# Two transformer layers on one core: where V's token tiles are projected, how the first chunk's reciprocal is cut, and where the second chunk's heads are split

## The chip, the cores and the metric

One Trainium2 chip, one of its cores. The metric is the device time of one launch in microseconds (us), the median of several runs; less is better. Engines are named as in the profile: PE is TensorE, DVE is VectorE, ACT is ScalarE, POOL is GpSimd, SP is SyncE.

## The reference

The input x is 2048 tokens by 512, in float32. The same two blocks are applied twice, with the same weights (two layers):

```
x = x + A(layernorm(x))     # A: q,k,v = x @ wqkv (32 heads of 16); softmax(q k^T / 4) v; @ wo
x = x + B(layernorm(x))     # B: mish(x @ w1 + b1) @ w2, hidden width 1792
```

Weights are wqkv 512 x 1536, wo 512 x 512, w1 512 x 1792, w2 1792 x 512, all float32.

## The kernel before

**Numbers.** Products with weights are made of three float32r matmuls each (`mm3`, L196 to L201): the operands are split into a high and a low half, and high x high, high x low and low x high are added up. A tile of 128 tokens by 512 outputs thus takes 4 x 3 matmuls of 128x512.

**Stages of a layer.** (1) `qkv` (L555) projects Q and K, feature tile by feature tile, for four chunks of 512 tokens, and writes them to DRAM (`scr`); from there `prep_qk` (L341) loads the rows of four heads at a time into the blocks `ks` and `qs`. Then it projects V (`v_parts`, L619): 16 tiles of 128 tokens, each in 4 parts (one for each 128 rows of the weight, three matmuls). Two tiles share a block `v` that GpSimd presets to 1 (L624), ScalarE evicts into it (L638), and SyncE writes each tile to DRAM (`vscr`, L642, 512 KB). `prep_v` (L370) loads the V rows of a group of four heads from there into `va`, in four pieces. (2) The attention (`Attention.run`, L506). (3) Output projection, the residual and the second layer norm. (4) The MLP. Activations between the layers lie in DRAM.

**The attention.** 512 steps (and 4 more to empty the pipeline): 8 groups of 4 heads, 4 chunks of 512 queries, 16 tiles of 128 keys. A step's scores are four 128x512 matmuls with 50 rows: 48 for the three-part product and 2 that subtract the row maximum. Scores are taken in threes: a pair (P: L452, one exponential of 128x1024 at L453) and a single (S: L462, exponential of 128x512 at L463). The row maxima are made ahead of the scores: a half max step (M, `max_mm`, L378) is two 128x512 matmuls into a pair of PSUM banks (`pm`, L400) and a DVE maximum over 128x1024 (L404). After each 16 max steps `max_fold` (L408) folds them: two small DVE operations (L413, L417), two GpSimd casts (high and low half, L421, L423), two writes to DRAM by SyncE (`nd`, L422, L424) and four transfers from there into the rows of `qs` (L427). The scores of those 16 steps need these rows. Small v in the cycle below is a pv matmul group (L478). Three steps make a cycle:

```python
CYCLE = ("PMvSM", "PvMSPMv", "SMPvMS")
```

PE's order is pinned as one chain. DVE, ACT, POOL and SP issue in order too; calls under `behind` keep program order there, the rest is placed by the scheduler. The maxima run `AHEAD` = 21 steps ahead of the scores. To get there, `qkv` runs `AHEAD + PRE` = 25 max steps between its matmuls (`some_max`): 12 in the Q/K part, 13 behind each third V part. It projects V's tiles 0 to 11 (48 parts); tiles 12 to 15 (16 parts) are projected by the attention itself in the first `2 * PRE` = 8 M places, two parts in each (L523), which are steps 0 to 3. The order of M places ends 21 steps before the scores; from there the tail runs without maxima.

**Blocks.** One pool of 22 blocks of 8 KB a partition holds nearly everything: weights, transposed inputs, `ks`, `qs`, `va`, `v`, the probabilities `p` (one block for a pair and a single), and, in the tail, the numerators and reciprocals. A block is given to its next owner in turn, so that an owner waits for the readers of the one before.

**Weights kept.** In layer 0, at step `KEEP` = 2, `keep_all` writes the six split blocks of wqkv to DRAM through GpSimd's queue (L144, 1 MB each), for layer 1.

**The end of the attention.** `HeadsOut` works on one chunk of 512 queries at a time: `load` brings numerator and denominator back from DRAM (L661), `invert` takes the reciprocal of the denominator (128x128, DVE, L664) and writes it out (POOL, L666), `spread` loads it over the heads' rows into the block `rec` (POOL, L672), `parts` multiplies (DVE, 128x2048, L676), casts the high half (POOL, L679) and subtracts for the low half (DVE, L680). The schedule at L886 hangs these on steps, counted from the end: chunk 0 at -42 (load), -38 (invert), -36 (spread), -20 (parts); chunk 1 at -29, -21, -20, -13; chunk 2 at -13, -9, -8. Behind the attention (L897 to L920) come the load of chunk 3, `parts` of chunk 2, and the output projections (`wo_parts`, L698) of chunks 0, 1, 2, with the layer norm of chunk 0 between them.

Of the kernel before, what the change touches and what calls it, by code (L numbers as in the profile page):

```python
# [38 lines left out]
QW = CW // 4  # L39
TR = 32  # L40
AHEAD = 21
PRE = 4
KEEP = 2
PREP = 2
WARM = (4, 1, 1)
# [1 line left out]
STEPS = NG * GSTEPS  # L47
# [31 lines left out]
def kernel(ctx: ExitStack, tc: tile.TileContext, x, wqkv, wo, w1, b1, w2, out):  # L79
# [48 lines left out]
    def behind(ins):  # L128
        return tc.keep_in_program_order(ins)
# [194 lines left out]
    class Attention:  # L324
# [181 lines left out]
        def run(self, hooks, pre):  # L506
            self.prep_v(0, range(NCH - 1))
            left = 2 * PRE
            close_banks()
            with tc.tile_pool(name="sa", bufs=1, space=PSUM, reuse_waits="tile") as self.pool:  # L510
                half, done = 2 * (AHEAD + PRE), -4
                for s in range(STEPS + 4):
                    if s % GSTEPS == GSTEPS - NKT and s // GSTEPS + 1 < NG:
                        self.prep_v(s // GSTEPS + 1)
                    for item in CYCLE[s % 3]:
                        if item == "P":
                            self.pair()
                            self.drain()
                        elif item == "S":
                            self.single()  # L520
                        elif item == "M" and left:
                            left -= 1
                            next(pre)  # L523
                            next(pre)
                            if not left:
                                next(pre, None)
                                self.prep_v(0, [NCH - 1])
                        elif item == "M":
                            self.max_mm(half // 2, half % 2)
                            half += 1  # L530
# [24 lines left out]
    def qkv(l, att, wts, tt, order, within, due):  # L555
        scr = att.scr
        ahead = [0]

        def some_max():
            if ahead[0] < AHEAD + PRE:  # L560
                for n in range(2):
                    att.max_mm(ahead[0], n)
                ahead[0] += 1

        done = 0
        spare = []
        parts = iter(())
        for n, (m, c) in enumerate(order):
            for fn in within.get((n, 0), []):
                fn()  # L570
            w = wts[m // 2]
            if n % 2:
                if not spare:
                    two = b8([P, 2, 2, CW], F32R, f"pt{l}{m}{c}")
                    spare += [two[:, 0], two[:, 1]]
                pt = spare.pop(0)
            else:
                pt = tmp.tile([P, 2, CW], F32R, tag="raw", name=f"pt{l}{m}{c}", bufs=3)
# [17 lines left out]
            split_psum(pt[:, 0], pt[:, 1], acc)  # L596
            nc.scalar.dma_start(
                scr[m][:, :, ts(c, CW)].bitcast(F32).rearrange("a p n -> p a n"), pt.bitcast(F32)
            )
            for fn in due.get((m, c), []):  # L600
                fn()
            for _ in range(2):
                next(parts, None)
            if m in (0, 4):
                done += 1
                if done == 2 * NCH:
                    parts = att.prep_qk(0)
# [11 lines left out]
    def v_parts(l, c, wts, tt, att, paired):  # L619
        th, tl = tt[c]  # L620
        for t in range(NCH):
            if t % 2 == 0:
                v = b8([P, 2, H, VW], F32, f"v{l}{c}{t}")
                nc.gpsimd.memset(v, 1.0)  # L624
                if paired:
                    pair = ps.tile([P, 2, 512], F32, tag="mx", name=f"vp{l}{c}{t}")
            acc = pair[:, t % 2] if paired else pbank("s", f"va{l}{c}{t}")
            for k in range(KT):
                w = wts[4 + k // 2]
                mm3(  # L630
                    acc,
                    [(th[:, k, ts(t, P)], tl[:, k, ts(t, P)], w[:, 0, k % 2], w[:, 1, k % 2])],
                    first=k == 0,
                    last=k == KT - 1,
                    pe=att.pe,
                )
                yield
            nc.scalar.activation(v[:, t % 2, :, 0:DH], acc.rearrange("p (h d) -> p h d", d=DH), AF.Copy)  # L638
            if t % 2:
                k0 = c * NCH + t - 1  # L640
                for k in range(2):
                    nc.sync.dma_start(  # L642
                        att.vscr[:, :, k0 + k].rearrange("g p n -> p g n"),
                        v[:, k].rearrange("p (g h) d -> p g (h d)", g=NG),
                    )

    class HeadsOut:
        def __init__(self, l, c, src):
# [11 lines left out]
            for h in range(P // DH):  # L660
                nc.sync.dma_start(self.num[ts(h, DH)], rows[:, h, 0:DH].rearrange("k d n -> d k n"))  # L661

        def invert(self):
            behind(nc.vector.reciprocal(self.den, self.den))  # L664
# [9 lines left out]
        def parts(self):  # L674
            nm = f"{self.l}{self.c}"
            behind(nc.vector.tensor_tensor(self.num, self.num, self.rec, op=ALU.mult))  # L676
            oh = b8([P, KT, CW], F32R, "oh" + nm)
            ol = b8([P, KT, CW], F32R, "ol" + nm)
            nc.gpsimd.tensor_copy(oh, self.num)  # L679
            behind(nc.vector.tensor_tensor(ol, self.num, oh.bitcast(F32), op=ALU.subtract))  # L680
            self.out = oh, ol

        def pieces(self):
            nm = f"{self.l}{self.c}"
# [149 lines left out]
    for l in range(2):  # L834
# [39 lines left out]
        def at(s, fn):  # L874
            hooks.setdefault(s, []).append(fn)
# [7 lines left out]
        for i in range(2):  # L883
            at(STEPS - 9 + 2 * i, lambda i=i: wot.append(ready(f"wo{i}", l)))
        outs = [HeadsOut(l, c, att.oscr) for c in range(NCH)]
        for c, (t0, t1, t2, t3) in enumerate(((-42, -38, -36, -20), (-29, -21, -20, -13), (-13, -9, -8, None))):  # L886
            o = outs[c]
            at(STEPS + t0, o.load)
            at(STEPS + t1, o.invert)
# [7 lines left out]
        att.run(hooks, v_parts(l, NCH - 1, wts, tt, att, True))  # L897
# [12 lines left out]
        for i, _ in enumerate(project(1)):  # L910
            for n in range({0: 1, 8: 1, 11: 2, 14: 2}.get(i, 0)):
# [70 lines left out]
```

## Time and profile before

| | |
|---|---|
| median of 3 runs | 3492.14 us (3491.93 to 3492.74) |
| the profiled execution's own time | 3493.51 us |
| its span | 3491.7 us, TensorE clock 1.00 |
| PE busy | 3478.3 us |
| DVE busy | 3001.3 us |
| ACT busy | 2572.9 us |
| POOL busy | 240.2 us |
| V stage of layer 0, layer 1 | 116.40 to 161.27, 1851.68 to 1896.56 |
| attention of layer 0, layer 1 begins | 161.27, 1896.56 |
| first output projection of layer 0 begins | 1400.68 |

All times of rows are microseconds from the span's start. A row of a timeline has start, duration, engine, line, operation, written and read tiles, shapes and count; in brackets stands the idle time of the engine ahead of it and what ended that. A row of the groups by line has count, busy time, mean duration in ns, idle time ahead and its main releasers. A matmul of 128x512 is shown longer than its share of TensorE, since matmuls are pipelined: the distance between starts counts. SPq is SyncE's sequencer issuing transfers.

### The profile page before, as it was taken

How to read it: one execution, taken by the hardware profiler on the slowest of the kernel's cores; microseconds unless marked ns; L12 is line 12 of the kernel's file. 1: busy time of each engine (PE TensorE's matmuls, PEld its weight loads, DVE VectorE, ACT ScalarE, POOL GpSimd, SP SyncE). 2: the span in 40 equal slices, each digit the busy share in tenths (PEclk: the TensorE clock that was granted, in tenths of full speed). 3: DMA queues.
4: the chain of work that ended last, by engine and by line, in shares of the span. 5: the costliest groups of instructions: out<-in, count | busy, mean ns of one | idle time of the engine just before them, and what ended most of it. 6: DMA issues, size and time to landing. Idle time of an engine off the chain costs nothing.

```text
span 3491.7 us, 68687 instructions
## 1 busy us (share of the span) xinstructions
PE 3478.3 (100%) x28572; PEld 1921.3 (55%) x28572; DVE 3001.3 (86%) x3166; ACT 2572.9 (74%) x3513; POOL 240.2 (7%) x392
## 2 busy tenths in 40 slices
PE   9999999999999999999999999999999999999999
PEld 7644444444444444888876444444444444448887
DVE  6689999999999996667756999999999999956675
ACT  3288888888888889356622888888888888884565
POOL 3100010001001002100010000000000000021000
PEclk9999999999999999999999999999999999999999
DMA  7741323222131314722374203111120312156210
GB/s 248 234 91 44 64 60 75 50 53 72 51 63 56 65 36 91 231 69 73 109 224 151 45 21 58 34 35 34 32 48 21 54 27 45 21 113 213 76 37 25
DMA packets 185268, 274.99 MB, mean 79 GB/s; under 512 B 72117, under 2 KB 114037, under 8 KB 171133
## 3 DMA queue, kind: packets, MB, share of 16 engines
q1 hardware_dynamic: 158036, 193.95, 22.8%
q10 hardware_dynamic: 19176, 43.06, 3.6%
q0 software_dynamic: 7744, 33.60, 3.4%
q8 instruction: 224, 3.67, 0.5%
q14 instruction: 88, 0.71, 0.1%
HBM read 158.87 MB, written 110.62 MB: 77 GB/s over the span
## 4 chain that ended last, share of the span: by engine, by line
PE 96%; DMA 1%; DVE 1%; ACT 1%; issue 0%; POOL 0%; SPq 0%; DVEq 0%; ACTq 0%; POOLq 0%
PE pv L478 30%; PE pm L400 18%; PE ss L462 13%; PE sp L452 9%; PE h L733 8%; PE mo L759 8%; PE qk L199 2%; PE qk L200 1%; PE qk L201 1%; PE va L199 1%; PE wo L199 1%; PE wo L201 1%; PE wo L200 1%; PE va L201 1%; PE va L200 1%; DMA vscr<-v 0%
## 5 line engine op out<-in xcount | busy, mean ns | idle before, releaser
L404 DVE TENSOR_REDUCE mxv<-pm 128x2 f32<-128x1024 f32 x2048 | 2384.2, 1218 | 148.4 <-PE pm L400 96.0
L453 ACT ACTIVATE p<-sp 128x1024 f32<-128x1024 f32 x1366 | 1396.5, 1022 | 10.6 <-DMA vscr<-v 2.7
L478 PE MATMUL pv<-p,va 128*32 128x256 f32 (+2 forms) x16032 | 1165.7, 392 | 0.6 <-ACT ot L501 0.4
L400 PE MATMUL pm<-ks,qs 48*128 48x512 f32 x4096 | 1099.0, 446 | 1.6 <-DVE mxv L404 1.3
L463 ACT ACTIVATE p<-ss 128x512 f32<-128x512 f32 x1364 | 815.3, 598 | 338.6 <-PE ss L462 258.1
L452 PE MATMUL sp<-qs,ks 50*128 50x512 f32 x2732 | 738.1, 445 | 0.5 <-ACT p L453 0.5
L478 PEld LDWEIGHTS pv<-p,va 128*32 128x32 f32 x16032 | 368.3, 108 | 504.9 <-issue 424.4
L400 PEld LDWEIGHTS pm<-ks,qs 48*128 48x128 f32 x4096 | 451.8, 184 | 347.2 <-issue 234.1
L462 PE MATMUL ss<-qs,ks 50*128 50x512 f32 x1364 | 610.6, 448 | 1.5 <-ACT p L463 1.5
L462 PEld LDWEIGHTS ss<-qs,ks 50*128 50x128 f32 x1364 | 252.1, 185 | 329.4 <-ACT p L463 238.1
L452 PEld LDWEIGHTS sp<-qs,ks 50*128 50x128 f32 x2732 | 267.0, 183 | 184.4 <-ACT p L453 108.5
L421 POOL CAST hi<-nt 128x32 fp32r<-128x32 f32 x64 | 13.3, 208 | 2263.1 <-DVE nt L417 2263.1
L736 ACT ACTIVATE hb<-h,b1t 128x512 f32<-128x512 f32 x112 | 77.2, 689 | 101.6 <-PE h L733 100.7
L740 ACT ACTIVATE hr<-he 128x512 f32<-128x512 f32 x112 | 70.8, 632 | 104.6 <-DVE he L739 104.6
L193 ACT ACTIVATE pt<-qk 128x512 fp32r<-128x512 f32 x64 | 38.2, 597 | 143.4 <-PE qk L201 102.0
L743 DVE TENSOR_TENSOR hb<-hb,hr 128x512 f32<-128x512 f32 x112 | 77.4, 691 | 45.0 <-ACT hr L741 42.9
L737 DVE TENSOR_SCALAR he<-hb 128x512 f32<-128x512 f32 x112 | 47.5, 424 | 79.8 <-ACT hb L736 73.8
L747 DVE TENSOR_TENSOR al<-hb,ah 128x512 fp32r<-128x512 f32 x112 | 77.4, 691 | 28.8 <-ACT ah L746 23.1
L746 ACT ACTIVATE ah<-hb 128x512 fp32r<-128x512 f32 x112 | 70.2, 627 | 29.9 <-DVE hb L743 29.9
L739 DVE SCALAR_TENSOR_TENSOR he<-he 128x512 f32<-128x512 f32 x112 | 76.7, 685 | 17.2 <-ACT he L738 17.2
L194 DVE TENSOR_TENSOR pt<-qk,pt 128x512 fp32r<-128x512 f32 x64 | 43.8, 685 | 53.7 <-ACT pt L193 51.6
L741 ACT ACTIVATE hr<-hr,lnhalf 128x512 f32<-128x512 f32 x112 | 81.1, 724 | 3.6
(224 smaller groups left out, 3000.5 us busy)
## 6 DMA issues: line engine op xcount, KB each, us to landing
scr<-pt ACTq DMA_DIRECT2D x64, 512.0 KB
qs<-scr SPq DMA_DIRECT2D x174, 128.0 KB
ks<-scr SPq DMA_DIRECT2D x174, 128.0 KB
vscr<-v SPq DMA_DIRECT2D x32, 512.0 KB
va<-vscr SPq DMA_DIRECT2D x64, 256.0 KB
oscr<-ot SPq DMA_DIRECT2D x64, 256.0 KB
ww<-sw POOLq DMA_DIRECT2D x14, 1024.0 KB, 4.3
num<-oscr SPq DMA_DIRECT2D x64, 128.0 KB
```

What stands on the lines that cost most here:

```text
L199: pe(nc.tensor.matmul(acc, ah, bh, start=first and i == 0, stop=False))
L200: pe(nc.tensor.matmul(acc, ah, bl, start=False, stop=False))
L201: pe(nc.tensor.matmul(acc, al, bh, start=False, stop=last and i == n - 1))
L400: nc.tensor.matmul(pm[:, e], qs[u][rows, q0 : q0 + P], ks[u][rows, ts(n, 512)], start=True, stop=True)
L404: nc.vector.tensor_reduce(self.mxs[b][:, 2 * u : 2 * u + 2, qt, n], pm, axis=AX.X, op=ALU.max)
L452: self.pe(nc.tensor.matmul(sp[:, e], k, q, start=True, stop=True))
L453: nc.scalar.activation(self.pts[-1][:, 0:n], sp[:, 0:n], AF.Exp, scale=SCALE)
L462: self.pe(nc.tensor.matmul(sp, k, q, start=True, stop=True))
L463: nc.scalar.activation(self.pts[i // 3][:, 2], sp, AF.Exp, scale=SCALE)
L478: nc.tensor.matmul(self.accs[b][ts(h, VW), cols], self.va[b // NCH][:, kt, h, :], self.pts[j][:, e, cols], start=kt == 0 and q0 == 0, stop ...
L733: pe(nc.tensor.matmul(acc, w[:, part, k, ts(f % 2, P)], t[:, k, :], start=i == 0, stop=i == 3 * KT - 1))
L759: nc.tensor.matmul(obs[c][t // 2][:, t % 2], act[:, ts(t, P)], w[:, part, f % 2], start=f == part == 0 and act is ah, stop=f == FT - 1 and ...
```

## The change

Three parts.

1. `PRE` goes from 4 to 1. The projections now take V's tiles 0 to 14 (60 parts); only tile 15 (4 parts) is left for the attention's first two M places. The maxima run 22 steps ahead in the projections instead of 25: 12 in the Q/K part, 10 in the V part, now behind each fourth part, which is a whole tile. In the attention, maxima therefore begin with the third M place. `v_parts` is one generator over all 16 tiles, evicts and writes a tile before it yields the last part, and takes its PSUM bank from the attention's pairs for tile 15 alone. From step 4 on the order of P, S, M and v is as before.
2. The reciprocal of chunk 0 is cut into four of 128x32, at steps -38 to -35; its writes to DRAM all go with the last; `spread` moves from -36 to -34.
3. `parts` of chunk 1 leaves step -13. Behind the attention come now: the product of chunk 1 and that of chunk 2 (both DVE), then the split of chunk 1 with its cast on ACT instead of POOL, and the subtraction on DVE. The split of chunk 2 (cast on POOL) follows in the middle of the first output projection.

```diff
-PRE = 4
+PRE = 1
...
-                            next(pre)
-                            next(pre)
+                            next(self.pre)
+                            next(self.pre)
                             if not left:
-                                next(pre, None)
                                 self.prep_v(0, [NCH - 1])
...
-        i = 0
-        for c in range(NCH - 1):
-            for _ in v_parts(l, c, wts, tt, att, False):
-                i += 1
-                if i % 3 == 0:
-                    some_max()
+        att.pre = v_parts(l, wts, tt, att)
+        for i in range(NKT * KT - 4 * PRE):
+            next(att.pre)
+            if i % 4 == 3:
+                some_max()
...
+    def v_parts(l, wts, tt, att):
+        for n in range(NKT):
+            c, t = divmod(n, NCH)
+            th, tl = tt[c]
             if t % 2 == 0:
                 v = b8([P, 2, H, VW], F32, f"v{l}{c}{t}")
                 nc.gpsimd.memset(v, 1.0)
-                if paired:
-                    pair = ps.tile([P, 2, 512], F32, tag="mx", name=f"vp{l}{c}{t}")
-            acc = pair[:, t % 2] if paired else pbank("s", f"va{l}{c}{t}")
+            if n < NKT - PRE:
+                acc = pbank("s", f"va{l}{c}{t}")
+            else:
+                acc = ps.tile([P, 2, 512], F32, tag="mx", name=f"vp{l}{c}{t}")[:, 0]
...
-        def invert(self):
-            behind(nc.vector.reciprocal(self.den, self.den))
-            for q in range(NCH):
+        def invert(self, i=0, n=1):
+            part = ts(i, P // n)
+            behind(nc.vector.reciprocal(self.den[:, part], self.den[:, part]))
+            for q in range(NCH if i == n - 1 else 0):
                 behind(nc.gpsimd.dma_start(self.rscr[:, ts(q, P)], self.den[ts(q, H)]))
...
-        for c, (t0, t1, t2, t3) in enumerate(((-42, -38, -36, -20), (-29, -21, -20, -13), (-13, -9, -8, None))):
+        for c, (t0, t1, t2, t3) in enumerate(((-42, -38, -34, -20), (-29, -21, -20, None), (-13, -9, -8, None))):
...
         outs[3].load()
-        outs[2].parts()
+        behind(outs[1].product())
+        behind(outs[2].product())
+        outs[1].split(nc.scalar)
...
-        for _ in project(0):
-            pass
+        for i, _ in enumerate(project(0)):
+            if i == NCH * KT // 2:
+                outs[2].split(nc.gpsimd)
```

`product` is the multiplication of `parts` alone, `split(engine)` the cast on the engine given and the subtraction on DVE.

More of the change, by code (lines that the diff above doesn't have):

```diff
@@ L504, in drain, with run @@
             self.stored = nc.sync.dma_start(self.oscr[qb][g // 2, g % 2], ot)
-        def run(self, hooks, pre):
+        def run(self, hooks):
             self.prep_v(0, range(NCH - 1))
@@ L636, in v_parts @@
                 )
-                yield
[L638 to L645, printed above, removed]
+                if k == KT - 1:
+                    nc.scalar.activation(v[:, t % 2, :, 0:DH], acc.rearrange("p (h d) -> p h d", d=DH), AF.Copy)
+                    for j in range(2 * (t % 2)):
+                        nc.sync.dma_start(
+                            att.vscr[:, :, n - 1 + j].rearrange("g p n -> p g n"),
+                            v[:, j].rearrange("p (g h) d -> p g (h d)", g=NG),
+                        )
+                yield
     class HeadsOut:
@@ L672, in spread, with product, split, parts @@
                 behind(nc.gpsimd.dma_start(self.rec[ts(h, DH)], rows[:, h][None].to_broadcast([DH, KT, CW])))
-        def parts(self):
+        def product(self):
+            return nc.vector.tensor_tensor(self.num, self.num, self.rec, op=ALU.mult)
+        def split(self, cast):
             nm = f"{self.l}{self.c}"
-            behind(nc.vector.tensor_tensor(self.num, self.num, self.rec, op=ALU.mult))
             oh = b8([P, KT, CW], F32R, "oh" + nm)
             ol = b8([P, KT, CW], F32R, "ol" + nm)
-            nc.gpsimd.tensor_copy(oh, self.num)
+            if cast is nc.scalar:
+                cast.activation(oh, self.num, AF.Copy)
+            else:
+                cast.tensor_copy(oh, self.num)
             behind(nc.vector.tensor_tensor(ol, self.num, oh.bitcast(F32), op=ALU.subtract))
             self.out = oh, ol
+        def parts(self):
+            behind(self.product())
+            self.split(nc.gpsimd)
         def pieces(self):
@@ L885 @@
         outs = [HeadsOut(l, c, att.oscr) for c in range(NCH)]
-        for c, (t0, t1, t2, t3) in enumerate(((-42, -38, -36, -20), (-29, -21, -20, -13), (-13, -9, -8, None))):
+        for c, (t0, t1, t2, t3) in enumerate(((-42, -38, -34, -20), (-29, -21, -20, None), (-13, -9, -8, None))):
             o = outs[c]
             at(STEPS + t0, o.load)
-            at(STEPS + t1, o.invert)
+            n = NCH if c == 0 else 1
+            for i in range(n):
+                at(STEPS + t1 + i, lambda o=o, i=i, n=n: o.invert(i, n))
             at(STEPS + t2, o.spread)
@@ L895, in project @@
             yield from wo_parts(l, c, outs, wot, x2s[c], att.pe)
-        att.run(hooks, v_parts(l, NCH - 1, wts, tt, att, True))
+        att.run(hooks)
         load_res(0)
         outs[3].load()
-        outs[2].parts()
+        behind(outs[1].product())
+        behind(outs[2].product())
+        outs[1].split(nc.scalar)
         load_res(1)
```

3 lines of the change are left out of this document (removed).

## The prediction

> **What bounds the kernel now.** I read the page's totals, its chain and its largest groups first, then the busy times by stretch, then the rows at the places that the diff touches.
>
> ```profile
> span 3491.7 us, 68687 instructions
> PE 3478.3 (100%) x28572; PEld 1921.3 (55%) x28572; DVE 3001.3 (86%) x3166; ACT 2572.9 (74%) x3513; POOL 240.2 (7%) x392
> PE 96%; DMA 1%; DVE 1%; ACT 1%; issue 0%; POOL 0%; SPq 0%; DVEq 0%; ACTq 0%; POOLq 0%
> L404 DVE TENSOR_REDUCE mxv<-pm 128x2 f32<-128x1024 f32 x2048 | 2384.2, 1218 | 148.4 <-PE pm L400 96.0
> ```
>
> TensorE is busy all through, and the chain that ends last is TensorE for 96%. The order of its matmuls is pinned, and the change issues the same matmuls: no term can come from less work. What can move is time in which TensorE stands at a matmul whose operand or bank isn't there, and the pace of a stretch whose mix isn't TensorE's own. The profiled execution took 3493.51 us, 1.8 around its span of 3491.7 and 1.4 above the median of 3492.14; I make the sum against it and take it off the median. A stretch of each stage (columns: window, its length, busy time and count of each engine, clock, DMA share, GB/s):
>
> ```profile
> 101.35:115.81 14.46, 14.46 (x67) 9.90 (x66) 11.81 (x12) 2.39 (x4) 1.81 (x1) 1.00 0.65 218
> 116.40:161.27 44.87, 44.76 (x198) 29.88 (x197) 33.88 (x31) 6.62 (x12) 12.66 (x13) 1.00 0.62 199
> 122.07:154.33 32.26, 32.26 (x145) 21.00 (x145) 26.36 (x24) 4.78 (x8) 10.52 (x9) 1.00 0.52 152
> 161.27:165.31 4.04, 4.04 (x16) 2.47 (x16) 0.00 (x0) 2.14 (x3) 0.00 (x0) 1.00 1.02 422
> 165.31:179.84 14.53, 13.71 (x58) 7.85 (x58) 0.00 (x0) 7.64 (x11) 0.00 (x0) 1.00 0.82 287
> 1851.68:1896.56 44.88, 44.77 (x198) 29.88 (x196) 33.88 (x31) 6.61 (x12) 4.02 (x4) 1.00 0.52 153
> 1900.60:1914.46 13.86, 13.47 (x59) 7.78 (x58) 0.00 (x0) 7.74 (x11) 0.00 (x0) 1.00 0.48 134
> 1302.00:1309.20 7.20, 7.20 (x74) 3.27 (x73) 6.98 (x7) 6.14 (x9) 0.00 (x0) 1.00 0.91 144
> 1314.80:1322.95 8.15, 7.48 (x74) 3.27 (x74) 8.01 (x9) 6.21 (x8) 2.48 (x6) 1.00 0.07 15
> 1400.68:1411.57 10.89, 10.89 (x52) 9.03 (x49) 6.41 (x4) 0.00 (x0) 1.90 (x1) 1.00 0.75 200
> ```
>
> In order: four Q/K tiles with their max steps; V's 48 parts in layer 0; eleven of its groups (three parts and a max step); step 0 of the attention; its steps 1 to 3; the V stage and steps 1 to 3 of layer 1; three steady steps; the three steps with the first reciprocal; the 48 matmuls of the first output projection. Layer 1's step 0 spans 1896.56 to 1900.60, the same 4.04.
>
> **The change part by part. 1, V's tiles.** The prices: 48 matmuls in 10.89 us make a part (three) 0.68 and a tile (twelve) 2.72. A Q/K tile with its max step takes 14.46/4 = 3.615, a V group 32.26/11 = 2.933, so a max step costs 0.89 by either (3.615 - 2.72, 2.933 - 2.04). The stage now is 13 groups and 9 bare parts, 13 x 2.933 + 9 x 0.68 = 44.25, measured 44.87. Afterwards it is ten tiles each with a max step, then five tiles bare: 10 x 3.615 + 20 x 0.68 = 49.75. Some 0.4 of today's 0.6 over the sum is VectorE's lag behind the Q/K tiles at the first groups, which a tile of 2.72 between maxima lets go. I take **+5.15 in each layer** (up to 5.5).
>
> In the attention, step 0 is a pair, a single and four V parts both before and after, 4.04. Steps 1 to 3 lose their 12 V parts (12 x 0.68 = 8.2 of TensorE) and get six half max steps. What they take then no row shows. From above, the steady 7.20, which has all pv matmuls where these have few. From below, 5.78, the pace that ScalarE's exponentials alone set where no maxima run (rows under 3: 1.445 from pair to pair). Between them lie six reduces, 4 in 4.55 back to back by the row at 1319.72 (under 2), 1.138 each and 6.8 in all, with two of them free to end after the stretch. I take 6.6. Layer 0: 14.53 to 6.6 is -7.9, with +5.15 **-2.8**. Layer 1: 13.86 to 6.6 is -7.25, **-2.1**. The 0.67 between the layers is this wait in layer 0, which goes: ScalarE held for a block that V's write had not yet left.
>
> ```profile
> 173.89 1.02 ACT L453 ACTIVATE p<-sp 128x1024 f32<-128x1024 f32 x1 [2.74 <-DMA vscr<-v]
> 181.60 2.36 DVE L404 TENSOR_REDUCE mxv<-pm 128x2 f32<-128x1024 f32 x2 [24.44 <-PE pm L400]
> ```
>
> The second row says why anything is to be had: VectorE idles 24.44 us there, though its reduces take 6.8 of each steady 7.20. Afterwards it works in that gap.
>
> What is late next? The row maxima. Six keep DMAs of the weights (L144, 1 MB each), V's writes (0.5 MB a tile) and the transfers of the folded maxima (L422 to L427) share the engines. SyncE issues in order.
>
> ```profile
> 134.19 1.15 SPq L427 DMA_DIRECT2D qs<-nd  x4
> 153.26 3.21 POOL L144 DMA_DIRECT2D wqkv<-sqkv  x6
> q0 software_dynamic: 831, 6.03, 90.5%
> q1 hardware_dynamic: 995, 0.51, 10.4%
> q1 hardware_dynamic: 4224, 2.21, 52.8%
> ```
>
> The last three are packets, MB and share of engines: the first two of 156 to 172 us, the third of 138 to 152. With the keep DMAs running, SyncE's queue gets 0.51 MB in 16 us, 0.03 a us; without, 2.21 MB in 0.528 x 14 us, 0.30. Today the four qs transfers are issued at 134.19, 27 us before the first scores at 161.27, and the keep DMAs behind the eighth block memset at 153.26. Afterwards the eighth memset waits only for tiles 2 and 3, written by about 135, so the keep DMAs begin near 137 and run to about 154 (6.3 MB at 6.03/16). In SyncE's order the low half of the maxima then stands behind GpSimd's six issues, and the qs transfers behind the writes of tiles 10 and 11, evicted at about 159. Tiles 4 to 9, some 2.6 MB, are still unwritten at 154; with tiles 10 and 11 it is 3.6 MB at 0.30 to 0.35, so qs lands at 164.5 to 168 and the first scores are wanted at 161.27 + 5.15 = 166.4. From 0 to 3 us; I take **+1.0, layer 0 alone**. Layer 1 keeps no weights.
>
> **2, the first reciprocal in four.**
>
> ```profile
> 1318.32 0.22 DVE L413 TENSOR_REDUCE folded<-mxv 128x16 f32<-128x64 f32 x1
> 1318.65 0.21 DVE L417 STREAM_TRANSPOSE nt<-folded 128x32 f32<-128x32 f32 x1
> 1318.85 0.95 DVE L664 RECIPROCAL den<-den 128x128 f32<-128x128 f32 x1
> 1319.72 4.55 DVE L404 TENSOR_REDUCE mxv<-pm 128x2 f32<-128x1024 f32 x4
> 1320.94 0.50 PE L400 MATMUL pm<-ks,qs 48*128 48x512 f32 x2 [0.67 <-DVE mxv L404]
> ```
>
> The reciprocal stands right behind a fold, 0.53 + 0.87 = 1.40 of VectorE between two reduces; TensorE waits, and the three steps take 8.15, 0.95 over the steady 7.20. So 0.45 is absorbed. A piece of 32 columns no row shows. From rows of other operations:
>
> ```profile
> L743 DVE TENSOR_TENSOR hb<-hb,hr 128x512 f32<-128x512 f32 x112 | 77.4, 691 | 45.0 <-ACT hr L741 42.9
> L680 DVE TENSOR_TENSOR ol<-num,oh 128x2048 fp32r<-128x2048 f32 x6 | 13.8, 2292 | 13.1 <-POOL oh L679 10.9 <-PE ss L462 2.1
> ```
>
> (2292 - 691)/1536 is 1.04 ns a column and 0.157 fixed; so a piece is 0.157 + 0.793/4 = 0.355, and as the reduce above began 0.08 before the reciprocal's end, it holds VectorE 0.275. It lies between 0.24 (a quarter) and 0.355. Slack is (7.20 - 6.83)/3 = 0.12 a step. The lag is then 0.53 + 0.275 in the first step and grows by 0.155 in three more, 1.27 at its height, less 0.45: 0.82 lost instead of 0.95, so -0.13. If the pieces fall into gaps, -0.7. I take **-0.2 a layer**. [...] The spread goes two steps later; its product, at step -20, is far off.
>
> **3, the second chunk's product and split behind the attention.**
>
> ```profile
> 1374.36 2.29 DVE L676 TENSOR_TENSOR num<-num,rec 128x2048 f32<-128x2048 f32 x1 [8.51 <-DMA oscr<-ot]
> 1375.13 0.60 ACT L463 ACTIVATE p<-ss 128x512 f32<-128x512 f32 x1
> 1376.73 1.02 ACT L453 ACTIVATE p<-sp 128x1024 f32<-128x1024 f32 x1 [1.00 <-DVE num L676]
> 1378.30 0.50 PE L462 MATMUL ss<-qs,ks 50*128 50x512 f32 x1 [0.75 <-ACT p L463]
> 1359.25 1.02 ACT L453 ACTIVATE p<-sp 128x1024 f32<-128x1024 f32 x1
> 1360.69 1.02 ACT L453 ACTIVATE p<-sp 128x1024 f32<-128x1024 f32 x1
> 3111.93 1.02 ACT L453 ACTIVATE p<-sp 128x1024 f32<-128x1024 f32 x1 [1.01 <-DVE num L676]
> ```
>
> In the tail the maxima have ended and ScalarE paces: 1.445 from pair to pair. At 1376.73 an exponential waits 1.00 for the block of `rec` that this product reads, and TensorE 0.75; layer 1 has the same wait. Without the product there the block isn't reused at that point: its place is taken by an old probability block. ScalarE makes up a little afterwards, so I take **-0.8 a layer** (nothing if the next block is late in turn; 1.0 at most).
>
> Behind the attention:
>
> ```profile
> 1402.24 2.29 DVE L676 TENSOR_TENSOR num<-num,rec 128x2048 f32<-128x2048 f32 x1 [0.73 <-DMA rec<-rscr]
> 1404.74 1.90 POOL L679 CAST oh<-num 128x2048 fp32r<-128x2048 f32 x1 [8.55 <-issue]
> 1406.67 2.29 DVE L680 TENSOR_TENSOR ol<-num,oh 128x2048 fp32r<-128x2048 f32 x1 [2.14 <-POOL oh L679]
> 1408.88 1.22 DVE L718 TENSOR_TENSOR x<-wo,x 128x1024 f32<-128x1024 f32 x1
> ```
>
> VectorE gets product 1 from 1401.5, product 2 to 1406, split 1 to 1408.3, while ScalarE, idle, casts beside product 2. The second projection begins at 1400.68 + 10.89 = 1411.6, so 3 us of cover. Split 2 then ends near 1412, before the third projection at 1422.5. The adds wait at most as long as today. I take 0; if the recs of chunk 2 land over 3 us later than at 1402.24, split 1, which stands behind product 2, holds TensorE for the rest.
>
> **The sum.** Layer 0: -2.8 + 1.0 - 0.2 - 0.8 = -2.8. Layer 1: -2.1 - 0.2 - 0.8 = -3.1. Together -5.9: 3493.5 becomes 3487.6, the median **3486.2**.
>
> **The rivals.**
> A, the row maxima are the new wait, and longer: each us that qs lands after 166.4 is a us. For it: the 0.03 MB a us. Against: the keep DMAs should end before tiles 10 and 11 are evicted. At 4 to 9 us it gives 3489 to 3494. It becomes slower than before where the keep DMAs begin as late as today, near 153: then tiles 8 to 11 stand behind them until 173, 2.1 MB at 0.30 go to 180, and qs lands near 181, 14.5 late: -6.9 + 14.5 = +7.6, **3499.7**. The point from which it decides: qs landing after 173.3 costs more than everything saved.
> B, the V tiles only change place and the tail's wait moves to the next block: steps 1 to 3 at 7.2, the stage at +5.5, -0.8 gone: 3486.2 + 1.2 + 0.7 + 1.6 = 3489.7. For it: ScalarE sat at its bound in the tail. Against: VectorE's 24 us of idle.
> C, more is won: steps 1 to 3 at 5.8 (-1.6), no qs wait (-1.0), the pieces in gaps (-1.0): 3482.6. For it: pv matmuls are few in these steps.
>
> **How the numbers follow.** The forecast 0.46 (3484 to 3489); A within 0.2% 0.16; A slower 0.08; B 0.10; C 0.20. A measurement of this kernel can tell about 0.2%, 7.0 us, from no change: faster is below 3485.2. C and a third of the forecast make 0.35, A's slow case 0.08, the rest 0.57. The range from 3482.0 to 3491.5 leaves out A's slow case, half of A and a little of C.
>
> **What would show it.** Right: the V stage about 50 us long, VectorE's first reduce in the attention within 3 us of its start instead of 24; steps 1 to 3 near 6.6; no idle ahead of the exponentials at step 501; the steps with the pieces near 8.0. Wrong: TensorE idle ahead of the first sp in layer 0 by more than 3 us, put to the qs transfers; a new wait in the tail; idle ahead of the second projection; maxima in steps 1 to 3 ahead of which TensorE waits for VectorE.

## The result, and the profile after

The changed kernel takes 4090.82 us in the median of 6 runs (3708.35 to 4419.95), the kernel before 3492.64 (3491.93 to 3493.33). The ratio 1.0618, with an interval of 1.0601 to 1.0636, is taken from the changed kernel's shortest runs alone (3708.4); the longer ones belong to it just as much, since by their spans and clocks the runs differ in how long TensorE's clock was halved. Seven executions are known, the profiled one among them: 3708.4 to 3708.8 (three, mean granted clock 0.935), 3766.1 (0.918), 4415.5 to 4420.0 (three, 0.76). The kernel before ran at 0.999 to 1.00 wherever its clock was read.

The page of the changed kernel, an execution of 3766.12 us:

```profile
span 3764.3 us, 68691 instructions
PE 3750.4 (100%) x28572; PEld 2029.4 (54%) x28572; DVE 3024.4 (80%) x3172; ACT 2585.1 (69%) x3515; POOL 240.3 (6%) x390
...
PEclk9955699999999999999997555899999999999999
...
L404 DVE TENSOR_REDUCE mxv<-pm 128x2 f32<-128x1024 f32 x2048 | 2398.9, 1219 | 395.3 <-PE pm L400 336.0
```

The first two lines hide it: TensorE is "100% busy" in both kernels, with the same 28572 matmuls. The third tells it: the granted clock drops in slices 3 to 5 and 25 to 29 of 40. VectorE's maxima take no longer (1219 ns against 1218), they wait for TensorE 336 us instead of 96.

Where exactly? The two fences show the V stage and then windows around the drop and the return in layer 0, and the same in layer 1 (window, length, busy time and count of PE, PEld, DVE, ACT, POOL, clock, DMA share, GB/s). The windows are 3.41 us long because the granted clock of these traces changes by that step: between two changes lie, in every profiled run here, whole multiples of 3.413 us, for the falls 1, 21, 80, 100, 101 and 616 of them (in this run 273.07 us, 80.0 of them, and 341.33 us, 100.0).

```profile
115.84:165.80 49.96, 49.96 (x222) 35.91 (x220) 26.83 (x25) 8.40 (x15) 12.57 (x13) 1.00 0.86 291
...
168.55:171.96 3.41, 2.71 (x15) 1.54 (x14) 1.23 (x1) 2.42 (x4) 0.00 (x0) 1.00 0.89 273
171.96:175.37 3.41, 2.56 (x16) 1.08 (x12) 3.07 (x3) 3.05 (x5) 0.00 (x0) 1.00 0.41 125
175.37:178.78 3.41, 3.41 (x23) 1.38 (x25) 2.21 (x3) 1.84 (x3) 0.00 (x0) 0.50 0.24 62
...
445.03:448.44 3.41, 3.41 (x17) 0.98 (x13) 2.45 (x2) 1.51 (x2) 0.00 (x0) 0.50 0.00 0
448.44:451.85 3.41, 3.41 (x36) 1.54 (x36) 2.50 (x3) 3.04 (x5) 0.00 (x0) 1.00 0.21 79
```

```profile
2028.81:2032.23 3.42, 2.44 (x18) 0.94 (x17) 3.42 (x4) 3.16 (x5) 0.00 (x0) 1.00 0.42 111
2032.23:2035.64 3.41, 3.41 (x27) 1.49 (x23) 2.03 (x2) 1.93 (x3) 0.00 (x0) 0.50 0.00 0
2370.15:2373.56 3.41, 3.41 (x16) 1.35 (x15) 1.62 (x2) 1.91 (x3) 0.00 (x0) 0.50 0.00 0
2373.56:2376.97 3.41, 3.41 (x37) 1.59 (x36) 3.01 (x4) 2.77 (x4) 0.00 (x0) 1.00 0.88 202
```

The clock is halved at 175.37 and back at 448.44, 273.1 us; in layer 1 from 2032.23 to 2373.56, 341.3 us. Both drops come about 1 us into step 3 of the attention (it begins at 174.75 and 2030.98), behind steps 1 and 2, the stretch that lost most of V's parts. These are TensorE's rows there:

```profile
170.42 0.40 PE L462 MATMUL ss<-qs,ks 50*128 50x512 f32 x1
171.51 0.50 PE L452 MATMUL sp<-qs,ks 50*128 50x512 f32 x2 [0.70 <-ACT p L453]
171.85 0.40 PE L400 MATMUL pm<-ks,qs 48*128 48x512 f32 x2
172.09 0.41 PE L462 MATMUL ss<-qs,ks 50*128 50x512 f32 x1
172.09 0.64 PE L400 MATMUL pm<-ks,qs 48*128 48x512 f32 x2
173.13 0.50 PE L452 MATMUL sp<-qs,ks 50*128 50x512 f32 x2 [0.41 <-ACT p L453]
173.58 0.50 PE L400 MATMUL pm<-ks,qs 48*128 48x512 f32 x2
173.92 0.39 PE L462 MATMUL ss<-qs,ks 50*128 50x512 f32 x1
174.75 0.50 PE L452 MATMUL sp<-qs,ks 50*128 50x512 f32 x2 [0.45 <-ACT p L453]
175.09 0.39 PE L400 MATMUL pm<-ks,qs 48*128 48x512 f32 x2
```

Only matmuls of 48 to 50 of the 128 rows are left, TensorE waits for ScalarE at each pair, and no pv has begun. In the window from 171.96 start 12 of them: 12 x 49/128 = 4.6 full-array matmuls of 128x512, where 3.41/0.227 = 15 fit (0.227 us each between starts, the 10.89 us for 48 of the first output projection in the kernel before, though a row shows 0.39). In layer 1's window before the drop, from 2028.81, start 9 such matmuls and the first 8 of pv. In the kernel before, in the window at the same place, 6 matmuls of V's parts and 5 of scores start, 8.0 by the same count:

```profile
171.89:175.30 3.41, 2.90 (x12) 1.60 (x11) 0.00 (x0) 1.41 (x3) 0.00 (x0) 1.00 1.06 321
```

What the falls cost, from the starts of the score pairs: steps 3 to 72 of layer 0 took 286.5 us and steps 3 to 120 of layer 1 433.0, against 166.5 and 282.6 in the filled kernel below, whose clock holds: 120.0 + 150.5 = 270.5 of the 272.6 us between the two profiled spans. The other 2.1 are 9.8 lost against the kernel before in steps 72 to 474 of layer 0 (5.1) and 120 to 474 of layer 1 (4.7), put down to the folds below, less some 7.7 gained.

Theory T, my guess from these counts (4.6 full matmuls where the clock fell, 8.0 where it held): the granted clock is halved when too little of TensorE's array works in one window, and the attention's own mix at half clock does too little to lift it again. The first expectations below still say it in terms of idle time, half a window of it, where the trace has TensorE busy for 2.56 of 3.41 us; the thin fill parts the two. R1: the reworked ends do it. R2: the load of the other engines and queues does it.

### The profile page after: what moved, and what is told of

It reads as the page before. It is cut to its first block, busy times and chain, and to the rows that moved or that the text cites. A ratio compares the mean times of both kernels' runs of the same rounds, so it can differ in the third digit from the quotient of the medians.

```text
span 3764.3 us, 68691 instructions
## 1 busy us (share of the span) xinstructions
PE 3750.4 (100%) x28572; PEld 2029.4 (54%) x28572; DVE 3024.4 (80%) x3172; ACT 2585.1 (69%) x3515; POOL 240.3 (6%) x390
## 4 chain that ended last, share of the span: by engine, by line
PE 94%; DVE 4%; ACT 1%; issue 0%; DMA 0%; POOL 0%; DVEq 0%; SPq 0%; ACTq 0%; POOLq 0%
PE pv L478 30%; PE pm L400 18%; PE ss L462 11%; PE sp L452 9%; PE h L742 8%; PE mo L768 8%; DVE mxv L404 3%; PE qk L199 1%; PE qk L200 1%; PE qk L201 1%; PE va L199 1%; PE wo L199 1%; PE wo L201 1%; PE wo L200 1%; PE va L201 1%; PE va L200 1%
## 5 line engine op out<-in xcount | busy, mean ns | idle before, releaser
L404 DVE TENSOR_REDUCE mxv<-pm 128x2 f32<-128x1024 f32 x2048 | 2398.9, 1219 | 395.3 <-PE pm L400 336.0
L478 PE MATMUL pv<-p,va 128*32 128x256 f32 (+2 forms) x16032 | 1290.4, 427 | 0.4 <-ACT ot L503 0.2
L400 PE MATMUL pm<-ks,qs 48*128 48x512 f32 x4096 | 1236.9, 484 | 2.0
L452 PE MATMUL sp<-qs,ks 50*128 50x512 f32 x2732 | 837.1, 469 | 3.5 <-ACT p L453 3.5
L400 PEld LDWEIGHTS pm<-ks,qs 48*128 48x128 f32 x4096 | 524.5, 201 | 416.6 <-issue 207.5
L478 PEld LDWEIGHTS pv<-p,va 128*32 128x32 f32 x16032 | 390.4, 114 | 581.0 <-issue 506.8
L462 PE MATMUL ss<-qs,ks 50*128 50x512 f32 x1364 | 660.3, 484 | 0.0
L462 PEld LDWEIGHTS ss<-qs,ks 50*128 50x128 f32 x1364 | 275.6, 202 | 368.7 <-ACT p L463 194.7
L452 PEld LDWEIGHTS sp<-qs,ks 50*128 50x128 f32 x2732 | 361.9, 204 | 170.1 <-ACT p L453 100.7
```

Source lines behind the costliest of these rows:

```text
L400: nc.tensor.matmul(pm[:, e], qs[u][rows, q0 : q0 + P], ks[u][rows, ts(n, 512)], start=True, stop=True)
L404: nc.vector.tensor_reduce(self.mxs[b][:, 2 * u : 2 * u + 2, qt, n], pm, axis=AX.X, op=ALU.max)
L452: self.pe(nc.tensor.matmul(sp[:, e], k, q, start=True, stop=True))
L462: self.pe(nc.tensor.matmul(sp, k, q, start=True, stop=True))
L478: nc.tensor.matmul(self.accs[b][ts(h, VW), cols], self.va[b // NCH][:, kt, h, :], self.pts[j][:, e, cols], start=kt == 0 and q0 == 0, stop ...
```

## The experiments

**Part 1 alone.** The changed kernel with parts 2 and 3 undone:

```diff
-        for c, (t0, t1, t2, t3) in enumerate(((-42, -38, -34, -20), (-29, -21, -20, None), (-13, -9, -8, None))):
+        for c, (t0, t1, t2, t3) in enumerate(((-42, -38, -36, -20), (-29, -21, -20, -13), (-13, -9, -8, None))):
...
-            n = NCH if c == 0 else 1
+            n = 1
...
-        behind(outs[1].product())
-        behind(outs[2].product())
-        outs[1].split(nc.scalar)
+        outs[2].parts()
...
-        for i, _ in enumerate(project(0)):
-            if i == NCH * KT // 2:
-                outs[2].split(nc.gpsimd)
+        for _ in project(0):
+            pass
```

> Part 1 alone (V's tiles, PRE 1), the ends of the attention as before. Theory T (TensorE's clock is halved because steps 1 to 3 of the attention, without V's parts and before the first pv matmuls, leave TensorE idle for half of one of the clock's windows; the attention's own mix cannot lift it again for 80 windows and more): the granted clock falls as in the changed kernel, 0.76 to 0.94 over the run, 3700 to 4420 us. Rival R1 (the drop comes from the reworked ends, parts 2 and 3): clock 1.00 and about 3497 us. By either, all 64 folds have their two VectorE steps next to each other, where before had a maximum between them in 40; that costs about 0.25 us each, 10 us in all, wherever the clock is full.

Four runs: 3502.1, 3649.8, 3651.6 and 3799.5 us, clock 0.999, 0.952, 0.952 and 0.909. The clock falls without the reworked ends, so R1 is out; the falls were shorter than expected, and only one run lies between 3700 and 4420. In the profiled run (3649.8) the clock fell in both layers, in layer 0 for one window of 3.41 us, in layer 1 for 101. Its window from 1909.98 holds scores and maxima alone, 4.6 full matmuls again. The run of 3502.1 shows what is left when the clock holds at 0.999: 9.3 us over the 3492.79 of the kernel before, where the folds cost 11.6 (below) and part 1 saves some.

**Parts 2 and 3 alone**, on the kernel before with PRE 4.

> Parts 2 and 3 alone (the reciprocal in four, the second chunk's split behind the attention), V's tiles as before. Theory T: clock 1.00 and about 3489.6 us: -0.8 a layer at step 501, -0.3 and -0.6 at steps 474 to 477. Rival R1 (these parts drop the clock): 0.76 to 0.94 and over 3700 us. The folds keep a maximum between their steps in 40 places, so no 10 us are lost.

3491.45 us (3490.22 to 3491.92, 10 runs), ratio 0.9995 (0.9986 to 1.0005), clock 1.00: 1.3 us less than before, and 1.9 more than expected. By the starts of the pairs, steps 474 to 480 take 15.04 us in both layers instead of 15.44 and 15.42, and steps 501 to 504 5.77 instead of 6.59 in both: -2.4 us in all. The projections behind the attention give back 0.2 and 0.5.

**The thin stretch filled.** Matmuls whose results are thrown away stand at the empty pv places of steps 1 and 2, 2, 2 and 3 of them:

```diff
+FILL = (0, 2, 2, 3)
...
                             done += 1
+                            if done <= 0:
+                                self.fill(FILL[done + 3])
                             self.pv(units(done))
...
+        def fill(self, n):
+            th, w = self.dense
+            for _ in range(n):
+                acc = pbank("acc", f"fill{self.l}{self.idle_no}")
+                self.idle_no += 1
+                self.pe(nc.tensor.matmul(acc, th[:, 0, 0:P], w[:, 0, 0], start=True, stop=True))
...
+        att.dense = tt[NCH - 1][0], wts[5]
```

> The changed kernel, with 2, 2 and 3 full-array 128x512 matmuls (results thrown away) at the three places of steps 1 and 2 where a pv group would stand but has no work yet. Theory T: TensorE is busy in that window, the clock stays 1.00, and the time is about 3495 us (the sum: V and first steps -4.8, reciprocal -0.9, step 501 -1.6, folds +10.3). Rival R2 (the drop comes from the load of the other engines and the DMA queues at that time, not from TensorE's idleness): the clock falls all the same, 3700 us and more. [...]

3489.26 us (3488.60 to 3492.70, 10 runs), ratio 0.9991 (0.9982 to 1.0000). In the profiled run no attention lost the clock, and no run was over 3492.7. More work on TensorE took some 220 us and more away, so R2 is out too. The 10 us for the folds were not lost: in this kernel the scheduler put the maximum back between their steps in 40 places.

**PRE 2**, otherwise the changed kernel: the fill is then V's own tile 14.

> The changed kernel with PRE 2: two V tiles instead of one in the attention, so 8 parts in the first four M places (step 0 and most of step 1). Theory T: the thin stretch is some 3 us instead of 5, shorter than a window of 3.41 us; the clock stays at 1.00 or falls less often, and at a full clock the time is about 3493 us (20 of the folds' maxima are back in between). Rival R2: falls as in the changed kernel, over 3700 us.

3492.23 us (3491.27 to 3493.35, 10 runs), ratio 0.9998 (0.9989 to 1.0007), clock 1.00. The folds are apart in layer 0 and together in layer 1 here, and each layer has its own pace: 115.8 us for 48 steps in layer 0, 116.4 in layer 1.

**Folds together in the kernel before.** Only the order of VectorE changes: the transposition is held right behind the reduction.

```diff
-            nc.vector.tensor_reduce(self.mxs[b][:, 2 * u : 2 * u + 2, qt, n], pm, axis=AX.X, op=ALU.max)
+            red = nc.vector.tensor_reduce(self.mxs[b][:, 2 * u : 2 * u + 2, qt, n], pm, axis=AX.X, op=ALU.max)
+            if self.turn:
+                follow(red, self.turn)
+                self.turn = None
...
-            nc.vector.tensor_reduce(
+            first = nc.vector.tensor_reduce(
...
-            nc.vector.transpose(nt, nm)
+            self.turn = follow(nc.vector.transpose(nt, nm), first)
```

> The kernel before, with one thing changed: the two VectorE steps of every fold (the reduction and the transposition) are held next to each other, where the scheduler had put a maximum between them in 40 of 64. If that order is what costs 0.62 us per 48 steps in the changed kernel, the same shows here: 116.4 instead of 115.8 per 48 steps, 3492.8 + 10 = about 3503 us, clock 1.00. If the loss comes from something else in the moved V tiles, about 3493.

3506.09 us (3505.78 to 3506.96, 5 runs) beside 3494.47, ratio 1.0034 (1.0022 to 1.0046): 11.6 us, from the order of two operations of 0.2 us in 40 places, 0.29 us each. The clock stayed at 1.00, so this order alone doesn't halve it. VectorE's rows at such a fold, in the kernel before:

```profile
585.74 0.21 DVE L413 TENSOR_REDUCE folded<-mxv 128x16 f32<-128x64 f32 x1
585.87 1.21 DVE L404 TENSOR_REDUCE mxv<-pm 128x2 f32<-128x1024 f32 x1
587.00 0.20 DVE L417 STREAM_TRANSPOSE nt<-folded 128x32 f32<-128x32 f32 x1
587.23 14.30 DVE L404 TENSOR_REDUCE mxv<-pm 128x2 f32<-128x1024 f32 x12
```

and in the changed kernel, where all 64 are like this:

```profile
702.68 0.22 DVE L413 TENSOR_REDUCE folded<-mxv 128x16 f32<-128x64 f32 x1
703.00 0.21 DVE L417 STREAM_TRANSPOSE nt<-folded 128x32 f32<-128x32 f32 x1
703.14 12.90 DVE L404 TENSOR_REDUCE mxv<-pm 128x2 f32<-128x1024 f32 x11
```

Together, the transposition stands still until its input is there (0.10 from the end of the reduction to its start), and both sit between two maxima: 0.46 from the start of the reduction to the next maximum. Apart, they push the maxima by 0.13 and 0.23, with a maximum between. The steady steps leave VectorE 0.37 us in three (7.20 less 6 x 1.138). A fold with its steps together exceeds that and holds TensorE up; but the excess is 0.09 us by this sum, and 0.29 is measured, so the order is shown as the cause and its price isn't explained.

**PRE 2 with the folds apart** (the transposition held behind the next maximum).

```diff
+            if self.turn:
+                b0, first, self.turn = *self.turn, None
+                follow(red, first)
+                self.max_turn(b0, red)
...
+            if b < NG * NCH - 1:
+                self.turn = b, first
...
```

`max_turn` is the rest of the fold, with its transposition held behind the operation given.

> PRE 2, with a maximum held between the two steps of every fold but the last of a layer. The kernel with PRE 2 took 3492.2 with 20 of them; a fold with its steps together costs about 0.2 to 0.3 us, so 40 more should save 8 to 12: 3480 to 3484 us. If the order of the folds doesn't matter: 3492. The clock stays at 1.00, as with PRE 2.

3487.94 us (3487.62 to 3489.08, 11 runs) beside 3494.47, ratio 0.9982 (0.9973 to 0.9991): 6.5 us below the kernel before. The gain from the order is smaller than expected: 48 steps, from step 96 on, take 115.8 to 116.4, no better than the 115.8 to 116.1 of the kernel before with two folds of three apart. So every third fold seems to cost nothing either way.

**The fill with a sixteenth of the array**: 32 rows and 32 columns instead of 128 and 128, folds together as in the changed kernel.

```diff
-                self.pe(nc.tensor.matmul(acc, th[:, 0, 0:P], w[:, 0, 0], start=True, stop=True))
+                self.pe(nc.tensor.matmul(acc[0:32], th[0:32, 0, 0:32], w[0:32, 0, 0], start=True, stop=True))
```

> The filled kernel, but the thrown-away matmuls use 32 rows and 32 columns of the array instead of 128 and 128, for the same 512 columns of data each. If what counts for the clock is the time in which TensorE streams (theory T1), the clock stays at 1.00 and the time is that of the filled kernel plus 10 for the folds, which stand together here: about 3499 us. If it is the share of the array that works (T2), these add a sixteenth, the window stays as poor as in the changed kernel, and the clock falls: over 3640 us.

Four runs: 3621.7, 4445.8, 4448.6 and 4490.9 us, clock 0.96 for the first and 0.75 for the others. The clock falls, as T2 (the share of the array that works) had it and T1 (the time in which TensorE streams) had not. The profiled run, at the drop in layer 0:

```profile
171.10:174.52 3.42, 3.31 (x16) 1.38 (x16) 1.57 (x2) 2.84 (x4) 0.00 (x0) 1.00 0.83 249
174.52:177.93 3.41, 3.29 (x10) 1.19 (x12) 2.01 (x2) 1.80 (x3) 0.00 (x0) 0.50 0.29 79
```

TensorE is busy for 3.31 of 3.42 us and the clock falls all the same. The 11 matmuls of scores and maxima that start in it and the four thin ones make 11 x 49/128 + 4/16 = 4.5 full matmuls. VectorE's folds stand together here and apart in the filled kernel, but the kernel before kept its clock with them together.

**A burst**: the changed kernel with 96 dense 128x128 matmuls (bfloat16, 128 columns of data each) at step 15 of each attention.

```diff
+    dense = const.tile([P, P], BF16, name="dense")
+    nc.gpsimd.memset(dense, 0.5)
...
+        def burst(self):
+            for i in range(2):
+                sp = ps.tile([P, 2, 512], F32, tag="mx", name=f"burst{self.l}{i}")
+                for e in range(48):
+                    self.pe(nc.tensor.matmul(sp[:, e % 2, 0:P], dense, dense, start=True, stop=True))
...
+                    if s == BURST:
+                        self.burst()
```

> The changed kernel with a burst of 96 dense 128x128 matmuls (thrown away) at step 15 of each attention, some 60 us after the clock has fallen. If a full window of dense work brings the clock back (T), each fall ends there: about 25 us lost and 8 for the burst in each layer, 3540 to 3580 us, clock 0.98. If a fall lasts for a set time whatever runs (rival: a timer of 80 windows or more), it changes nothing: 3700 to 4420 us.

Four runs: 3501.8, 3525.0, 3551.3 and 3551.4 us, clock 0.999, 0.992 and twice 0.983. The slowest two were at half clock for 2 x 0.017 x 3550 = 121 us, the third for 2 x 0.008 x 3523 = 56. From the drop to the burst it is about 50 to 55 us at half clock, and the burst's first window comes on top, so this is one such stretch for the third run and two for the slowest, and the times go by steps of 23.2 and 26.3 us. That fits falls that end at the burst; no trace shows one, since the profiled run is the one of 3501.8. There the clock held in layer 0 and came back by itself after one window in layer 1. The folds have their maximum back between them in 40 places here too.

**PRE 3 with the folds apart**, and **three matmuls of fill** (FILL = (0, 1, 1, 1)) with PRE 1 and the folds apart.

> As the kernel with PRE 2 and the folds apart (0.9982 of before), but PRE 3: three V tiles in the attention. If what PRE does beside the clock is to move a V tile from a slow place (steps 0 to 3) to a cheaper one, each tile kept in the attention costs about 1 us a layer: 0.9985 to 0.999 of before, between PRE 2 and before. If PRE 2 is already past the best point: below 0.998. Clock 1.00 by either, with richer windows than PRE 2.

> PRE 1 with the folds apart and three thrown-away dense matmuls (one at each empty pv place of steps 1 and 2) instead of seven. By the share of the array that works in one window, counted from the matmuls' shapes, windows of 0.28 to 0.31 have fallen and windows of 0.33 and more in the attention have not; three matmuls bring the poorest from 0.29 to about 0.38, so the clock should hold (T2), and the time be 0.7 us a layer below the filled kernel: 0.998 to 0.9985 of before. If three are too few, the clock falls in some runs, over 3600 us there.

Side by side, with before at 3492.99: PRE 3 3487.37 us (3486.44 to 3488.58), ratio 0.9984 (0.9975 to 0.9993); the fill 3486.19 us (3484.91 to 3488.23), ratio 0.9982 (0.9973 to 0.9991), 11 runs each, clock 0.999 to 1.00. These two and PRE 2 (0.9982) can't be told apart, so what a V tile kept in the attention costs stays open. The window at the thin stretch of the kernel with three matmuls of fill:

```profile
171.60:175.02 3.42, 3.34 (x16) 1.46 (x16) 2.76 (x3) 3.35 (x5) 0.00 (x0) 1.00 0.63 185
```

It is as busy as the one with thin matmuls (3.34 against 3.31) and has two dense matmuls and 12 of scores and maxima starting in it, 6.6 full ones.

## Why the prediction was wrong

It forecast 3486.2 us. The step that failed is the first: "no term can come from less work. What can move is time in which TensorE stands at a matmul whose operand or bank isn't there, and the pace of a stretch whose mix isn't TensorE's own." I had read the clock of 1.00 in every row as a constant. In the changed kernel it fell to 0.50 behind the two stretches that had lost dense work, for 614.4 of 3764.3 us. The 12 V parts in steps 1 to 3 were work, and they were also what filled the array until the pv matmuls began. My own lower bound for those steps, 5.78 at ScalarE's pace, described the danger, and I priced only its time. None of the rivals had it, and the slower side of the result came by none of their roads.

Shown by runs: part 1 makes the fall, parts 2 and 3 don't; dense matmuls in the stretch prevent it, thin ones that keep TensorE busy don't. That a dense burst ends it fits the times and clocks of four runs. The time for which TensorE is busy didn't tell when it fell or came back: the changed kernel's clock fell with no gap over 0.70 us, a window with 97% busy fell in the thin fill (3.31 of 3.42 us), and windows busy from end to end at half clock (3.41 of 3.41 us) didn't lift it for 80 in a row. The opposite is there too: in layer 0 of the burst kernel's profiled run the window from 170.93, with TensorE busy for 2.57 us, kept the clock, where the changed kernel's with 2.56 lost it; one V matmul and 12 of scores and maxima start in it, 5.6 full ones against 4.6.

What goes with the falls in these runs is the share of the array at work, and the profiled runs allow a finer count of it, an estimate of mine from the rows' shapes and starts. Take each matmul as its rows times columns over 128 x 128, times its columns of data over 512, and spread it over the time in which it streams, beginning 0.1 us behind its recorded start: 0.227 us for 512 columns of data, 0.43 at half clock. The pv matmuls, the transposes and the warm-up at the kernel's start are plain float32 and count twice, since their starts stand twice as far apart: four pv matmuls of 384 columns of data, side by side, take 0.35 us where 384/512 x 0.227 is 0.17, the transposes of 128 columns 0.109 where it is 0.057, the warm-up's of 512 columns 0.43 where it is 0.227. Then, over the 12 profiled runs from 5 us on:

| windows | number | full matmuls, of 15 |
|---|---|---|
| at full clock, and it fell inside the kernel | 8 | 3.0 to 5.5 |
| at full clock, and it fell as the kernel ended | 12 | 0 to 5.4 |
| at full clock, and it held | 11710 | 6.3 and more |
| at half clock, and it stayed | 913 | up to 6.0, and 908 of them up to 5.9 |
| at half clock, and it came back | 8 | 5.9 to 8.2 |

In these runs one border near 6 of 15 fits both ways, to within 0.1. By it the length of the falls can be read: at full clock a window of steady attention holds 36 or 37 matmuls, at half clock 16 to 27 (rows above), so the same mix at half clock does about half the work in a window, up to 6.0 by the count, and the falls ended at windows of 5.9 to 8.2. The border is an estimate from the table: the 0.1 us and the double weight of pv were chosen with the traces in view. With 0.05 to 0.2 us the falls stay apart from the rest; without any delay the highest fall (5.94) and the lowest window that held (5.85) overlap slightly, and with pv counted once they don't separate. Rows and columns were never varied apart, so whether cells or something near them are counted isn't shown.

The second step that failed was silent: I took VectorE's order outside the changed places as unchanged, a term put at nothing without a reason. The scheduler put the two steps of all 64 folds together, where 40 had been apart; that costs 11.6 us by itself in the kernel before, about twice the forecast gain of 5.9, so the changed kernel would probably have been slower even at full clock.

The terms of the sum were mostly close:

- V's stage: +5.15 a layer forecast; +5.09 and +5.08 from the first V matmul to the first scores.
- Steps 1 to 3: 6.6 forecast; 6.75 and 6.80 with the clock held (three matmuls of fill).
- The row maxima: +1.0 forecast, nothing measured. The keep DMAs start at 135.16 (137 forecast) and the qs transfers are issued at 160.21, where I had them, but the first scores start at 165.80 without a wait: 5.6 us were enough. The working itself gave no wait: 3.6 MB at 0.30 to 0.35 a us from 154 end at 164 to 166, not at up to 168, and 166.4 was wanted. Rows of the changed kernel's timelines, for this point and the next two:

```profile
135.16 1.12 POOL L144 DMA_DIRECT2D wqkv<-sqkv  x2
...
160.21 2.20 SPq L427 DMA_DIRECT2D qs<-nd  x4
...
1440.67 0.35 DVE L664 RECIPROCAL den<-den 128x32 f32<-128x32 f32 x1
1440.94 2.29 DVE L404 TENSOR_REDUCE mxv<-pm 128x2 f32<-128x1024 f32 x2
...
1498.50 1.02 ACT L453 ACTIVATE p<-sp 128x1024 f32<-128x1024 f32 x1
```

- The reciprocal: -0.2 a layer forecast, -0.40 and -0.38 measured (parts 2 and 3 alone). The piece has the forecast size, 0.35 and 0.27 to the next start. More of the lag was absorbed than I had reckoned. Each piece is dearer than a quarter of the whole (0.24) all the same: the first three take 0.35, 0.34 and 0.34, four such 1.4, against 0.95 for the whole.
- The wait at step 501: -0.8 a layer forecast, -0.82 measured; the exponentials run through at 1498.50.
- Behind the attention: 0 forecast, -0.3 to +0.5 in the kernels run.

With three matmuls of fill and all folds apart, the change's three parts give 3492.99 - 3486.19 = 6.8 us, where the sum had 5.9. The maxima's +1.0 that didn't come makes up the difference. So the sum was about right for a kernel whose clock and VectorE order stay, and the changed kernel keeps neither.

Still open: how long a fall lasts when nothing dense follows. It was 1, 80, 100 and 101 windows in the profiled runs of the changed kernel and of part 1 alone, 21 and 616 in the thin fill, the last to the end of the maxima. My guess from the count is that it depends on when the mix at half clock lines up with the windows; no run tests that. The falls aren't bound to the attention: the filled kernel's profiled run lost one window at its start (at 28.98, behind a window in which dense matmuls waited for data, with gaps of 0.99 and 0.76 us and 4.9 by the count).

## What to carry to other kernels

Work that looks movable from a thin stretch of TensorE may be what keeps its clock, as it was here: before moving dense matmuls away, count the full-array matmuls left in each window of 3.41 us there (by the estimated count the clock fell here at 3.0 to 5.5 of 15 inside the kernel and held at 6.3 and more), and read the granted clock of the result before any other line. "100% busy" tells neither: it stood on both pages. If a stretch gets thin, try a few thrown-away matmuls, or leave the last piece of real dense work there; here three of 0.227 us in each layer kept the clock at 0.999 to 1.00, where the changed kernel without them took 3708 to 4420 us, and the two ways came out alike (0.9982 each). And where a scheduler places operations, compare the order of every engine over the whole program, since an order that no edit touched can move by itself.

## What the runs showed of the hardware

At half clock the changed kernel's attention ran at 12.91 us for three steps instead of 7.20, with TensorE busy for 3.41 of 3.41 us. It stayed there for 80 and 100 windows of 3.413 us, part 1 alone for 1 and 101, the thin fill for 21 and 616 (2103 us). By the estimated count the clock came back at windows of 5.9 to 8.2 full-array matmuls of 15 and was lost at 5.5 and less. Runs of the changed kernel lay 710 us apart (3708 to 4420), at mean clocks of 0.935 and 0.76.

Two operations of 0.2 us on VectorE, the second dependent on the first, cost 11.6 us more (3506.09 against 3494.47) next to each other than with an independent maximum between them, in 40 places. Next to each other the second stood still for 0.10 us; that and the lost slack account for 0.09 of the 0.29 us at each place, and the rest is open.
